# Two attention layers on one core: three edits to the planner of the instruction order

## The chip, the core and the metric

The kernel runs on one core of a Trainium2 chip. The core has a matrix engine (TensorE, PE in the profile; its weight loads are PEld), a vector engine (VectorE, DVE), a scalar engine (ScalarE, ACT), a general engine (GpSimd, POOL) and a queue engine (SyncE, SP). Each takes its own instructions strictly in the order in which the program holds them, and waits where an operand or a buffer is not ready. DMA transfers are issued by SP, ACT and POOL and run beside the engines. The metric is the device time of one execution, in microseconds (us), the median of the runs shown.

## The reference

Two attention layers of their own inputs and weights, whose outputs are joined along the last axis. Both have 2048 rows, 1024 columns and 32 heads of 32.

```python
def _A_ref(x, wqkv, wo):          # layer A
    W, dil = 8, 2
    q, k, v = ...                 # x @ wqkv, by head
    idx = pos[:, None] - (jnp.arange(W) * dil)[None, :]
    logits = einsum(q, k[idx]) * Dh ** -0.5      # 8 keys, every second one back
    logits = where(idx >= 0, logits, -1e9)
    return (softmax(logits) @ v[idx]) @ wo

def _B_ref(x, wqkv, wo):          # layer B
    W = 256
    scores = einsum(q, k) * (Dh ** -0.5)
    mask = (i - j >= 0) & (i - j < W)            # the last 256 keys
    scores = where(mask, scores, -1e9)
    return (softmax(scores) @ v) @ wo

return concatenate([A, B], axis=-1)
```

## The kernel before

**Units.** Each layer is cut into four units of 512 rows. Units 0 to 3 are layer B (dense, `DU` = 4 of them), units 4 to 7 layer A, whose even and odd rows were parted on the host so that its window is eight neighbouring keys. Every unit has eight head groups of four heads. A number (u, s) is unit and head group; `hg` = 8u + s.

**Precision.** A factor of a projection is split into a rounded part and a remainder (`Stream.parts`, L276 on ScalarE or L279 on VectorE for the rounding, L282 on VectorE for the remainder), and three products of 512 columns are summed in a PSUM bank (`TERMS`). Tiles so made are called w (weights), x (inputs) and r (sums and outputs of heads). Their raw data come through three buffers `raw`, loaded by POOL (L221); a load waits until the split of the tile three places earlier has freed its buffer. `split_to(n)` issues the splits up to item n of one long list of items, and with them the next loads.

**Layer B, attention.** A first pass (`first`) makes scores of 128 rows by 384 keys in one of four rotating PSUM banks `s`; VectorE masks them and takes the largest (L1388), ScalarE sums the exponentials (`total`, L1393), and then the bank is free. After 16 such sums their logarithm (L1406), its split (L1411 to L1414) and a small transposing matmul of `hl` with `ident` (`rows`) give 32 extra rows that are written under the queries (L1428). The second pass (`second`) computes the scores again, transposed and already normed, in the same four banks; ScalarE takes the exponentials into `pbuf` (L1473), POOL or VectorE masks them (L1452, L1455), and matmuls with V (`o<-pbuf,vbuf`) follow. The Q and K blocks are evacuated into `nat` (L625 on ScalarE, L629 on VectorE) and copied by SP into two alternating stacks `qst` and `kst` (L649), as soon as the second pass of the head group before the last has left them.

**Layer A, attention.** Scores of 32 by 40 (`s<-pbuf`), a chain on VectorE (L1214 mask, L1224 largest, L1226 subtraction, L1238 to L1242 norm, L1244 transpose) with one exponential on ScalarE between (L1230), copies into `wide` (L1253, L1256), and matmuls with V.

**Layer A, values.** Units 6 and 7 take V by seven products of half matrices (`value_product`, in the plan as "vp"), which need sums of halves of x (`sx`, items of kind "xw") and of the weights (`tv`, kind "w"). Their parts are added in VectorE out of the PSUM banks `g` (L1007); three such banks rotate. Background work (`half_sums`, L1096 to L1106) prepares these sums with DMA and VectorE while earlier units run; it begins when the last dense head group is done.

**The order.** Nothing reorders instructions later: the program's order on every engine is what a planner issues. `Clock` keeps an estimated time for each engine. A loop takes the item that can start first from four lists (sums, second pass, first pass, and `gemm`, the projections in the order of `plan`), issues its matmuls and defers what follows to an estimated moment (`ck.defer(t, f)`): work deferred to an earlier moment is issued earlier, and so stands further ahead on its engine. `e` in `first` is the estimated end of L1388 as ScalarE sees it. While `ck.traced` is set, the clock estimates loads and POOL's starts by a second model; it is set between two places in `gemm`, `marks`. In a Q/K block `run(k)` is called for k = 0 to 7, each three matmuls, and decides at which k the next items are split.

Of the kernel before, what the change touches and what calls it, by code (L numbers as in the profile page):

```python
# [55 lines left out]
BANK_LATE = 0.0  # L56
# [235 lines left out]
def kernel(ctx, tc, xs, wqk, wv, wo, outs, units):  # L292
# [4 lines left out]
    DU = sum(u[2] for u in units)  # L297
# [18 lines left out]
    ck = Clock()  # L316
# [98 lines left out]
    for p in plan:  # L415
# [21 lines left out]
        else:  # L437
# [8 lines left out]
            else:  # L446
# [6 lines left out]
    st = Stream(nc, ck, raws, wpool, xpool, items, [more[:, 1024 * i:1024 * i + 1024] for i in range(3)],  # L453
                where[("qk",) + LIGHT_FROM + (0,)] if LIGHT_FROM[0] < U else len(items))
# [76 lines left out]
    xt, xready, ot, rows, waiting = {}, {}, {}, {}, {}  # L531
# [24 lines left out]
    rg, rs, ro = Ring(psg, 7 - NS, "g"), Ring(pss, NS, "s"), Ring(pso, 1, "o")  # L556
# [7 lines left out]
    def latest(*ts):  # L564
        return None if any(t is None for t in ts) else max(ts)


    def qk_items(u, s):
# [98 lines left out]
        for t in range(2):  # L667
            h = {}

            def ready(k, t=t, h=h):  # L670
                if k == 0:
                    st.split_to(where["qk", u, s, t] + 1)
                    w = st.ready[where["qk", u, s, t]]
                    h["r"] = w if isinstance(w, list) else [w, w]
                    return latest(rg.when(), h["r"][0], xready[u][0])
                if k >= len(xready[u]):
                    return None
                if k == NK - 1 and nat + t >= NN and (dense or t == 0):
                    n = done["nat"].get(nat + t - NN)
                    return n and max(xready[u][k], n - 0.6)  # L680
                return max(xready[u][k], h["r"][k // 4])

            def run(k, t=t, h=h):
                if k == 0:
                    h["ps"], h["b"] = rg.take()
                    h["w"], _ = st.get(where["qk", u, s, t])
                for i, (a, b) in enumerate(TERMS):
                    mm(h["ps"], h["w"][:, a, k * P:(k + 1) * P], xt[u][k][:, b, :],
                                     start=(k == 0 and i == 0), stop=(k == NK - 1 and i == 2))
                then = where["qk", u, s, t] + 1  # L690
                if t == 1 and s == 0 and u:
                    then = max(then, st.split)
                kinds = [kind for kind, _ in st.items[then:then + 2]]
                if k == ASK and kinds and kinds[0] not in ("x", "xw"):
                    st.split_to(then + 1)
                if k == ASK and t == 0 and u > DU and kinds[:1] == ["x"] and st.split >= where["qk", u, s, 1]:
                    st.split_to(where["qk", u, s, 1] + 1)
                if kinds[:1] == ["xw"] and k in (0, 2, 4, 6):
                    st.split_to(then + 1 + k // 2)
                if kinds == ["w", "w"] and k == 5 and (then in firsts or then + 1 in firsts):  # L700
                    st.split_to(then + 2)
                if kinds == ["w", "xw"] and k == 6:
                    st.split_to(then + 2)
                if k in (4, 6) and kinds[:1] == ["xt"]:
                    st.split_to(then + k // 2)
                if k == 6 and t == 1 and not hg:
                    st.split_to(7)

            def after(k, t=t, h=h):
                if k == NK - 1:  # L710
                    evac(t, h["ps"], h["b"])

            for k in range(NK):
                out.append((lambda k=k, ready=ready: ready(k), lambda k=k, run=run: run(k), 3 * CG,
                            lambda k=k, after=after: after(k)))
# [644 lines left out]
    def attention(u, s):  # L1360
# [11 lines left out]
        def first(b, j):  # L1372
            if "nm" not in h:
                h["nm"] = small.tile([P, 16], F32, tag="nm", name="nm")
                h["sm"] = small.tile([P, 16], F32, tag="sm", name="sm")
            full, mask = 384, cst["mask_d"]
            cut = 0 if has_halo else max(0, 256 - P * b)
            n = full - cut
            c1 = 256 + P * b + P
            c0 = c1 - n  # L1380
            i = j * 4 + b
            ps, bank = rs.take()
            mm(ps[:, :n], q[0:96, j, b * P:(b + 1) * P], kk[0:96, j, c0:c1],
                             start=True, stop=True)
            nm, sm = h["nm"][:, i:i + 1], h["sm"][:, i:i + 1]

            def top():
                nc.vector.tensor_tensor_reduce(ps[:, :n], ps[:, :n], mask[:, cut:full], scale=-1.0, scalar=BIG,  # L1388
                                               op0=ALU.add, op1=ALU.min, accum_out=nm)
                e = ck.use("dve", n / 960 + 0.114, ck.now) + 0.06  # L1390

                def total():
                    nc.scalar.activation(ps[:, :n], ps[:, :n], AF.Exp, bias=nm, scale=-1.0, accum_out=sm)  # L1393
                    e2 = ck.use("act", n / 1200 + 0.236, e)
                    rs.give(bank, e2)
                    h["left"] -= 1
                    if h["left"] == 0:
                        ck.defer(e2, log_sum)

                ck.defer(e - 0.1, total)  # L1400

            return top

        def log_sum():
            ln = small.tile([P, 16], F32, tag="ln", name="ln")
            nc.scalar.activation(ln, h["sm"], AF.Ln)  # L1406
            e = ck.use("act", 0.13, ck.now) - 0.03

            def parts():
                nl = small.tile([P, 16], F32, tag="nl", name="nl")  # L1410
                nc.vector.tensor_tensor(nl, h["nm"], ln, op=ALU.subtract)  # L1411
                hl = small.tile([P, 2, 16], F32R, tag="hl", name="hl")
                nc.vector.tensor_copy(hl[:, 0, :], nl)
                nc.vector.tensor_tensor(hl[:, 1, :], nl, hl[:, 0, :].bitcast(F32), op=ALU.subtract)  # L1414
                e2 = ck.use("dve", 0.52, e, port=True)
                aux.append(Item(lambda: latest(rs.when(BANK_LATE), e2), lambda: rows(hl), 0.08))

            ck.defer(e, parts)

# [131 lines left out]
    aux, ones, twos, gemm = [], [], [], []  # L1551
# [6 lines left out]
    x1 = None  # L1558
    marks = []
    for p in plan:  # L1560
        if not marks and p[1] >= DU:
            marks.append(len(gemm))
        if len(marks) == 1 and p[0] == "p":
            marks.append(len(gemm))
        if p[0] == "qk":
            new = qk_items(p[1], p[2])
            if p == ("qk", 0, 0):
                q, k, x = new[:NK], new[NK:], x_items(0)
                f = dict(FILL)
                new = x[0] + sum([q[i:i + 1] + fill(i + 1, f.get(i + 1, 0)) for i in range(4)], [])  # L1570
                for i in (1, 2, 3):
                    new[new.index(q[2 * i]) if i < 2 else len(new):0] = x[i]
                    if i == 1:
                        new += k[:4]
                    else:
                        new += q[2 * i:2 * i + 2] + k[2 * i:2 * i + 2]
            if p[1:] == (0, NG - 1):
                x1 = x1 or x_items(1)
                for g in range(3, FIRST_X - 1, -1):
                    new[NK + 2 * g - 2:NK + 2 * g - 2] = x1[g]  # L1580
            gemm += new
        elif p[0] == "v":
            new = v_items(p[1], p[2])
            if p[1:] == (0, 2) and FIRST_X:
                x1 = x_items(1)
                for g in range(FIRST_X - 1, -1, -1):
                    new[X1_AT[g]:X1_AT[g]] = x1[g]
            elif V_SLOTS.get(NG - 1) == p[2] and 0 < p[1] < U - 1:
                m = 2 * VPARTS[p[2]][1]
                for g, x in reversed(list(enumerate(x_items(p[1] + 1)))):  # L1590
                    new[m * g + XAT:m * g + XAT] = x
            gemm += new
        elif p[0] == "o":
            gemm += o_items(p[1], p[2])
        elif p[0] == "p":
            gemm += product(p[1], p[2])
        elif p[0] == "vp":
            new = value_product(p[2])
            if VP_AT.get((p[1], NG - 1)) == p[2:] and p[1] + 1 < U:
                for g, x in reversed(list(enumerate(x_items(p[1] + 1)))):  # L1600
                    new[4 * g + XAT:4 * g + XAT] = x
            gemm += new
# [87 lines left out]
```

## Time and profile before

| | |
|---|---|
| median of 3 runs | 1803.5 us |
| lowest and highest | 1801.02 and 1804.85 us |
| the profiled execution's own time | 1798.77 us |
| its span | 1796.8 us |
| layer B | about 0 to 1030 us of the span |
| layer A | Q/K of its first unit from about 970 us, products of values between 1330 and 1530 us, outputs to the end |

The profile is one execution. Views read in it: the page, the waits (which engine sat idle before an instruction, and whose end released it), the time line (start, duration, engine, line, tiles, and in brackets the idle time ahead), and stretches of time with each engine's busy time. An instruction of the new order has no time there; where it would fall is read from its neighbours on the matrix engine.

### The profile page before, as it was taken

Reading aid. Unit: us, or ns where it says so; the run is one execution under the profiler, and the core shown is the slowest. Engines: PE = TensorE matmul, PEld = TensorE weight load, DVE = VectorE, ACT = ScalarE, POOL = GpSimd, SP = SyncE. Lnnn points to the kernel's source line nnn. Section 1 sums busy time; section 2 is a strip of 40 time slices with the busy share of each in tenths; the row PEclk is TensorE's granted clock in tenths of the full one; section 3 lists DMA queues with packets and bytes.
Section 4 is the critical chain, followed back from the end, with each engine's and each line's share of the span. In section 5 each row is a group of like instructions: output and inputs, shape, how many; then the busy total and the mean of one; then the engine's idle time right before and its main releaser. Section 6 shows DMA issues by size and latency. Waiting matters only on the chain.

```text
span 1796.8 us, 38440 instructions
## 1 busy us (share of the span) xinstructions
PE 1774.0 (99%) x14496; PEld 1442.6 (80%) x14496; DVE 1297.5 (72%) x2877; ACT 943.7 (53%) x2337; POOL 411.8 (23%) x961
## 2 busy tenths in 40 slices
PE   9999999999999999999999999999999999999999
PEld 7787778888778888878787788888888787887887
DVE  6777876768867769867678556766666768868866
ACT  5565566555656555656554524543464435355442
POOL 3322323222332222332223400101010101001120
PEclk9999999999999999999999999999999999999999
DMA  8354664645645556555556166766576667848984
GB/s 257 106 147 136 185 167 136 166 136 145 185 141 161 152 134 169 152 146 149 145 134 185 48 202 197 226 204 186 183 226 192 198 196 254 291 139 280 346 280 144
DMA packets 154793, 324.57 MB, mean 181 GB/s; under 512 B 18032, under 2 KB 58992, under 8 KB 154608
## 3 DMA queue, kind: packets, MB, share of 16 engines
q0 software_dynamic: 45792, 166.74, 30.5%
q1 hardware_dynamic: 98736, 137.02, 26.8%
q10 hardware_dynamic: 10080, 18.35, 2.8%
q8 instruction: 115, 1.88, 0.4%
q14 instruction: 70, 0.57, 0.1%
HBM read 201.33 MB, written 53.48 MB: 142 GB/s over the span
## 4 chain that ended last, share of the span: by engine, by line
PE 88%; DVE 4%; DMA 3%; issue 3%; ACT 1%; SPq 0%; POOL 0%; DVEq 0%; ACTq 0%; POOLq 0%
PE g L324 69%; PE s L324 13%; PE o L324 6%; DVE w L282 1%; DMA raw<-xs 1%; DMA raw<-tv 1%; DMA kst<-nat 1%; ACT s L1393 0%; DMA pbuf<-nat 0%; DVE x L282 0%; ACT w L276 0%; DVE r L1101 0%; DVE band L1242 0%; DMA qst<-nat 0%; DVE w L279 0%
## 5 line engine op out<-in xcount | busy, mean ns | idle before, releaser
L324 PE MATMUL g<-x,w 128*128 128x512 f32 x3552 | 876.2, 393 | 2.2 <-DVE w L282 0.7
L324 PEld LDWEIGHTS g<-x,w 128*128 128x128 f32 x3552 | 656.5, 188 | 131.6 <-issue 5.8
L282 DVE TENSOR_TENSOR w<-raw,w 128x512 fp32r<-128x512 f32 x510 | 334.1, 697 | 53.8 <-ACT w L276 47.3
L1393 ACT ACTIVATE s<-s,nm 128x384 f32<-128x384 f32 (+2 forms) x512 | 274.3, 537 | 118.4 <-DVE nm L1388 112.0
L1388 DVE CUSTOM_DVE_ANT_0 s<-s,mask_d 128x384 f32<-128x384 f32 (+2 forms) x512 | 261.9, 554 | 90.5 <-PE s L324 90.2
L324 PE MATMUL g<-w,x 128*128 128x256 f32 (+1 forms) x1728 | 308.9, 327 | 3.3 <-DVE w L279 1.8
L1452 POOL TENSOR_SCALAR_AFFINE_SELECT pbuf<-pbuf 128x128 f32<-128x128 f32 (+1 forms) x604 | 218.8, 390 | 315.1 <-ACT pbuf L1473 313.5
L324 PEld LDWEIGHTS g<-w,x 128*128 128x128 f32 x1728 | 256.3, 191 | 29.2 <-DVE w L282 2.7
L324 PE MATMUL g<-r,w 128*128 128x512 f32 x960 | 238.2, 393 | 0.5 <-DVE r L1352 0.5
L1473 ACT ACTIVATE pbuf<-s 128x384 f32<-128x384 f32 (+2 forms) x480 | 203.7, 504 | 62.6 <-PE s L324 60.3
L324 PEld LDWEIGHTS g<-r,w 128*128 128x128 f32 x960 | 177.3, 188 | 35.9 <-DVE r L1352 1.1
L221 POOL DMA_DIRECT2D raw<-wqk x126 | 68.1, 540 | 359.4 <-DVE w L282 241.9
L324 PEld LDWEIGHTS s<-qst,kst 128*128 128x128 f32 x704 | 113.9, 189 | 42.5 <-ACT s L1393 17.4
L324 PE MATMUL s<-kst,qst 96*128 96x384 f32 (+2 forms) x512 | 143.0, 343 | 3.5 <-DMA kst<-nat 2.6
L324 PE MATMUL s<-qst,kst 128*128 128x256 f32 (+2 forms) x704 | 137.2, 302 | 4.0 <-ACT s L1393 3.2
L276 ACT CAST w<-raw 128x1024 fp32r<-128x1024 f32 (+1 forms) x89 | 92.0, 1038 | 67.0 <-PE g L324 29.9
L279 DVE CAST w<-raw 128x1024 fp32r<-128x1024 f32 x167 | 115.7, 693 | 15.7 <-PE g L324 10.5
L324 PEld LDWEIGHTS s<-kst,qst 96*128 96x128 f32 x512 | 93.9, 189 | 29.1 <-issue 7.6
L1393 ACT ACTIVATION_READ_ACCUMULATOR s<-s,nm 128x1 f32 x512 | 105.3, 206 | 0.0
L1253 ACT COPY wide<-band 32x512 f32<-32x512 f32 x128 | 79.0, 617 | 25.0 <-DVE band L1244 23.6
L324 PE MATMUL o<-pbuf,vbuf 128*32 128x384 f32 (+2 forms) x1408 | 91.1, 388 | 0.0
L282 DVE TENSOR_TENSOR x<-raw,x 128x512 fp32r<-128x512 f32 x116 | 75.6, 689 | 21.2 <-ACT x L276 19.9
(91 smaller groups left out, 1394.1 us busy)
## 6 DMA issues: line engine op xcount, KB each, us to landing
raw<-wqk POOLq DMA_DIRECT2D x126, 512.0 KB, 4.8
raw<-wv POOLq DMA_DIRECT2D x60, 512.0 KB, 5.1
qst<-nat SPq DMA_DIRECT2D x96, 256.0 KB, 3.1
kst<-nat SPq DMA_DIRECT2D x96, 256.0 KB, 4.8
raw<-wo POOLq DMA_DIRECT2D x44, 512.0 KB, 4.5
raw<-xs POOLq DMA_DIRECT2D x28, 512.0 KB, 4.6
outs<-ost ACTq DMA_DIRECT2D x38, 256.0 KB, 2.5
kst<-halo SPq DMA_DIRECT2D x72, 128.0 KB, 4.7
```

The source lines that it names most:

```text
L221: (self.nc.scalar if early else self.nc.gpsimd).dma_start(raw if len(ap.shape) == 2 else raw.rearrange("p (a b) -> p a b", a=2), ap)
L276: nc.scalar.copy(t[:, 0, :], raw)
L279: nc.vector.tensor_copy(t[:, 0, :], raw)
L282: nc.vector.tensor_tensor(t[:, 1, c:c + 512], raw[:, c:c + 512], t[:, 0, c:c + 512].bitcast(F32), op=ALU.subtract)
L324: nc.tensor.matmul(out, left, right, **k)
L1253: nc.scalar.copy(diag[r:r + 32, :, :, c:c + 32], turned[r:r + 32, :, :, 1, :])
L1388: nc.vector.tensor_tensor_reduce(ps[:, :n], ps[:, :n], mask[:, cut:full], scale=-1.0, scalar=BIG, op0=ALU.add, op1=ALU.min, accum_out=nm)
L1393: nc.scalar.activation(ps[:, :n], ps[:, :n], AF.Exp, bias=nm, scale=-1.0, accum_out=sm)
L1452: nc.gpsimd.affine_select(w, w, pattern=[[0, m], [step, n]], compare_op=ALU.is_ge, fill=0.0, base=base, channel_multiplier=chan)
L1473: nc.scalar.activation(w, ps[:, :pack * n].rearrange("p (j n) -> p j n", j=pack), AF.Exp)
```

## The change

```diff
@@ in qk_items, run(k) @@
-                if kinds[:1] == ["xw"] and k in (0, 2, 4, 6):
-                    st.split_to(then + 1 + k // 2)
+                if kinds[:1] == ["xw"] and k in (0, 2, 4):
+                    st.split_to(then + 2 + k // 2)
...
-                if kinds == ["w", "xw"] and k == 6:
+                if kinds == ["w", "xw"] and k == 3:
                     st.split_to(then + 2)
@@ in attention, first @@
-                ck.defer(e - 0.1, total)
+                ck.defer(e - 0.7, total)
@@ in attention, log_sum @@
-                aux.append(Item(lambda: latest(rs.when(BANK_LATE), e2), lambda: rows(hl), 0.08))
+                aux.append(Item(lambda: latest(rs.when(BANK_LATE), e2 + 0.4), lambda: rows(hl), 0.08))
@@ in the main part @@
-        if not marks and p[1] >= DU:
+        if not marks and p[1:] == (DU, 2) and p[0] == "qk":
             marks.append(len(gemm))
```

1. Ahead of a value product, the last Q/K block splits the product's items at k = 0, 2 and 4, two at the first of these, instead of one each at 0, 2, 4 and 6; where the next items are one weight and then such a sum, they are split at k = 3 instead of 6.
2. The summing exponential is deferred to 0.7 us ahead of the estimated end of L1388, instead of 0.1.
3. The transposing matmul of the sums may be issued 0.4 us later by the planner's clock.
4. The second model of the clock begins with the third Q/K block of unit 4, not with the first entry of the plan that belongs to that unit.

The matmuls are the same and as many. On ScalarE stand 14 instructions fewer than before, on VectorE 13 fewer, on POOL 27 more: casts and masks that the planner gave to another engine. SP's order is the same. The matrix engine's order is the same up to about 43 us, from about 1030 to 1405 us and from about 1550 us on; between these it differs in many places. Three follow, as the built programs hold them. Names are output<-inputs, with the numbers of the buffers.

**First place: a second pass of the dense layer beside the first pass of the next head group, at 448 to 455 us before (it comes again 256 us later in each dense unit).** The matrix engine, before:

```order
L324 MATMUL g_4881<-x_4855,w_4700 128x512 x3
L324 MATMUL g_4881<-x_4858,w_4700 128x512 x3
L324 MATMUL s_4955<-qst1_124,kst1_126 128x384
L324 MATMUL s_4957<-qst1_124,kst1_126 128x256 x2
L324 MATMUL s_4961<-qst1_124,kst1_126 128x256 x2
L324 MATMUL s_4965<-qst1_124,kst1_126 128x128 x2
L324 MATMUL s_4971<-qst1_124,kst1_126 128x128 x2
L324 MATMUL g_4985<-x_4704,w_4950 128x512 x3
L324 MATMUL s_4994<-kst0_125,qst0_123 128x384
```

and with the change:

```order
L324 MATMUL s_4932<-qst1_124,kst1_126 128x256 x2
L324 MATMUL g_4898<-x_4868,w_4712 128x512 x3
L324 MATMUL s_4946<-qst1_124,kst1_126 128x128 x2
L324 MATMUL s_4950<-qst1_124,kst1_126 128x128 x2
L324 MATMUL s_4954<-kst0_125,qst0_123 128x384
L324 MATMUL g_4898<-x_4871,w_4712 128x512 x3
L324 MATMUL s_4979<-kst0_125,qst0_123 128x384
L324 MATMUL s_4981<-kst0_125,qst0_123 128x384
L324 MATMUL s_4987<-kst0_125,qst0_123 128x384
L324 MATMUL s_4991<-kst0_125,qst0_123 128x384
```

The Q block's last product (g_4881, now g_4898) moved behind the second pass, and four first-pass matmuls follow it at once; s_4987 takes the bank of s_4950, and s_4991 that of s_4954. ScalarE there, before:

```order
L1473 ACTIVATE pbuf_110<-s_4929 128x384
L1473 ACTIVATE pbuf_110<-s_4932 128x384
L625 ACTIVATE nat_4943<-g_4881 128x512
L1393 ACTIVATE s_4897,sm_4643<-s_4897,nm_4642 128x384
L1473 ACTIVATE pbuf_110<-s_4955 128x384
```

and with the change:

```order
L1473 ACTIVATE pbuf_110<-s_4946 128x2x128
L625 ACTIVATE nat_4970<-g_4898 128x512
L1473 ACTIVATE pbuf_110<-s_4950 128x2x128
L1393 ACTIVATE s_4954,sm_4650<-s_4954,nm_4649 128x384
L1393 ACTIVATE s_4979,sm_4650<-s_4979,nm_4649 128x384
```

The evacuation L625 stands ahead of the summing exponential in both.

**Second place: VectorE ahead of the fifth value product, at 1422 to 1434 us before.** r_15951 and r_15954 (now r_15933 and r_15936) are the first sums of x, w_16012 (now w_15996) is the product's second weight. Before:

```order
L1224 TENSOR_REDUCE nm_15924<-band_10854 128x16
L1226 TENSOR_TENSOR band_10854<-band_10854,nm_15924 128x16x40
L1238 TENSOR_REDUCE sm_15940<-band_10854 128x16
L1240 RECIPROCAL sm_15940<-sm_15940 128x16
L1242 TENSOR_TENSOR band_10854<-band_10854,sm_15940 128x16x40
L1244 STREAM_TRANSPOSE band_10854<-band_10854 128x1024
L282 TENSOR_TENSOR r_15951<-raw_15759,r_15951 128x512
L282 TENSOR_TENSOR r_15954<-raw_15759,r_15954 128x512
L279 CAST w_15984<-raw_15821 128x1024
```

and with the change, from the second half of the first sums on:

```order
L282 TENSOR_TENSOR r_15936<-raw_15756,r_15936 128x512
L1224 TENSOR_REDUCE nm_15942<-band_10883 128x16
L1226 TENSOR_TENSOR band_10883<-band_10883,nm_15942 128x16x40
L279 CAST w_15966<-raw_15832 128x1024
L282 TENSOR_TENSOR w_15966<-raw_15832,w_15966 128x512 x2
L1238 TENSOR_REDUCE sm_15974<-band_10883 128x16
L1240 RECIPROCAL sm_15974<-sm_15974 128x16
L1242 TENSOR_TENSOR band_10883<-band_10883,sm_15974 128x16x40
L1244 STREAM_TRANSPOSE band_10883<-band_10883 128x1024
L282 TENSOR_TENSOR r_15982<-raw_15841,r_15982 128x512
L282 TENSOR_TENSOR r_15985<-raw_15841,r_15985 128x512
L282 TENSOR_TENSOR w_15996<-raw_15951,w_15996 128x512 x2
```

The split of the first sums moved from behind the window's softmax to ahead of it, and the first weight into its middle.

**Third place: ScalarE ahead of the last value product, at 1517 to 1525 us before.** w_17124 is that product's first weight. Before:

```order
L1326 COPY r_11650<-o_17077 128x512
L1037 DMA vd_108<-r_15148 128x512
L586 ACTIVATE nat_17105<-g_17041 128x512
L276 CAST w_17124<-raw_17048 128x1024
L1230 ACTIVATE band_11127<-band_11127 128x16x40
L591 COPY nat_17105<-g_17112 128x512
```

and with the change:

```order
L586 ACTIVATE nat_17083<-g_17035 128x512
L1037 DMA vd_108<-r_15148 128x512
L1326 COPY r_11650<-o_17093 128x512
L1230 ACTIVATE band_11132<-band_11132 128x16x40
L591 COPY nat_17083<-g_17113 128x512
```

The cast of w_17124 left ScalarE; it stands on VectorE now (L279), between L1226 and L1238 of the same window.

## The prediction

> **What bounds the kernel now.** I read the page's head first, then the waits of the matrix engine (PE), then the stretches of 100 us, then the time line at each wait.
>
> ```profile
> span 1796.8 us, 38440 instructions
> PE 1774.0 (99%) x14496; PEld 1442.6 (80%) x14496; DVE 1297.5 (72%) x2877; ACT 943.7 (53%) x2337; POOL 411.8 (23%) x961
> ```
>
> PE is busy for all but 22.8 us. The number of its instructions does not change, so a new order can win or lose only what PE waits, and the slow clock that follows some waits. The waits by releaser (total, times, longest):
>
> ```profile
> PE s L324 <- ACT s L1393: 4.5, 7, 1.0
> PE g L324 <- DVE w L282: 3.5, 7, 1.3
> PE s L324 <- DMA kst<-nat: 2.6, 1, 2.6
> PE g L324 <- DVE w L279: 1.8, 1, 1.8
> ```
>
> So four kinds carry it: score banks that ScalarE's summing exponential (L1393) holds, weight splits of VectorE in layer A, one key copy by DMA, one late cast. By stretch (PE, PEld, DVE, ACT, POOL, clock, DMA share, GB/s):
>
> ```profile
> 100.00:200.00 100.00, 98.17 (x584) 79.52 (x583) 78.96 (x218) 54.65 (x170) 30.06 (x72) 0.98 0.50 140
> 900.00:1000.00 100.00, 96.79 (x621) 81.41 (x621) 74.50 (x181) 51.97 (x151) 30.11 (x72) 0.98 0.52 140
> 1500.00:1600.00 100.00, 97.34 (x1189) 78.01 (x1188) 75.49 (x124) 47.47 (x89) 9.52 (x18) 1.00 0.75 251
> ```
>
> The worst stretches are the dense layer's first unit, the passage to layer A, and layer A's products of values: the three that the edits reorder.
>
> **A. The split of sums earlier (L698 to L703).** It adds no work; it issues the same splits of layer A's value products two to three steps of a Q/K block earlier, thus also the loads behind them. A 128x512 matmul takes 0.23 us from start to start (30 in 7.09 us in the first row). The products' waits:
>
> ```profile
> 1515.60 7.09 PE L324 MATMUL g<-x,w 128*128 128x512 f32 x30
> 1427.90 0.72 POOL L221 DMA_DIRECT2D raw<-wv  x1 [7.55 <-DVE r L282]
> 1431.93 1.05 ACT L276 CAST w<-raw 128x1024 fp32r<-128x1024 f32 x1 [0.56 <-DMA raw<-wv]
> 1433.03 0.50 PE L324 MATMUL g<-w,r 128*128 128x512 f32 x1
> 1434.36 1.88 PE L324 MATMUL g<-w,r 128*128 128x512 f32 x7 [0.83 <-DVE w L282]
> 1380.44 1.05 ACT L276 CAST w<-raw 128x1024 fp32r<-128x1024 f32 x1 [0.52 <-DMA raw<-tv]
> ```
>
> At 1433 us PE loses 1434.36 - 1433.03 - 0.23 = 1.1 us. The chain runs back to POOL: its load of the last weight waited 7.55 us for a buffer which the split of r (L282) frees, and VectorE had that split behind a whole softmax (reduce to transpose). In the new order it stands ahead of the first reduce, four softmax rows earlier, so the load leaves some 4 us sooner and the weight is no longer what is late; VectorE's last subtraction is, by about 0.3 us (it now stands behind the transpose). Saved: 0.8. At 1380 us the late thing is the landing of raw<-tv; its request keeps its place on POOL, so that wait stays.
>
> ```profile
> 1510.29 4.33 PE L324 MATMUL g<-x,w 128*128 128x512 f32 x18 [0.65 <-DVE r L1007]
> 1519.67 1.05 ACT L276 CAST w<-raw 128x1024 fp32r<-128x1024 f32 x1 [1.78 <-DMA raw<-tv]
> 1520.62 0.73 ACT L1230 ACTIVATE band<-band 128x640 f32<-128x640 f32 x1
> 1525.12 0.65 DVE L279 CAST w<-raw 128x1024 fp32r<-128x1024 f32 x1
> 1522.53 1.52 PE L324 MATMUL g<-w,x 128*128 128x512 f32 x6
> 1525.83 0.49 PE L324 MATMUL g<-w,x 128*128 128x512 f32 x1 [1.78 <-DVE w L279]
> 1526.55 1.67 PE L324 MATMUL g<-w,x 128*128 128x512 f32 x6 [0.23 <-DVE w L282]
> ```
>
> At 1510 PE waited 0.65 us for a bank that VectorE empties (L1007); that row moves ahead of the softmax: saved 0.7. At 1525 the loss is 1525.83 - 1522.53 - 6 x 0.23 = 1.9, then 1526.55 - 1525.83 - 0.23 = 0.5, so 2.4. Here ScalarE held the window's exponential (L1230) behind a cast that waited 1.78 us for DMA; in the new order the cast goes to VectorE and the exponential is free. VectorE's cast at 1525.12 then comes about 1.9 us sooner, but PE arrives 0.8 sooner too: 1.1 saved. What is late next is the same cast. A: -0.8 - 0.7 - 1.1 = -2.6; between 0 (the splits wait for landings all the same) and -4.2 (all three gone).
>
> **B. The passage to layer A.** The exponentials' move and the later switch of the planner's clock re-plan 930 to 1030 us; from there to 1370 us every engine's order is the old one, so the switch costs nothing in layer A itself.
>
> ```profile
> 966.60 0.72 POOL L221 DMA_DIRECT2D raw<-wv  x1 [2.12 <-DVE pbuf L1455]
> 968.81 2.61 SPq L649 DMA_DIRECT2D kst<-nat  x3
> 971.47 4.39 SPq L1096 DMA_DIRECT2D r<-wv  x4
> 974.00:976.00 2.00, 2.00 (x11) 1.65 (x10) 1.70 (x4) 0.97 (x4) 0.80 (x1) 1.00 1.10 225
> 982.45 1.22 PE L324 MATMUL s<-kst,qst 96*128 96x384 f32 x3 [2.60 <-DMA kst<-nat]
> 982.00:984.00 2.00, 1.55 (x5) 1.49 (x6) 1.94 (x4) 0.00 (x0) 0.30 (x1) 0.63 1.02 382
> 983.47 2.92 PE L324 MATMUL g<-w,x 128*128 128x512 f32 x7
> ```
>
> The last head's key copies are issued at 968.8 and land only at 982.4, because the DMA engines are full (share 1.10). PE waits 2.60 us; then the granted clock is 0.63 and seven matmuls take 2.92 instead of 1.6, 1.3 more: 3.9 in all. In the new order PE's work between the last use of the old keys and the first use of the new ones, counted in matmuls of the times above, is 13.8 us instead of 12.6, and two of the weight loads that share the engines are asked for some 4 us of PE work earlier. If the copies land as late as now relative to their issue, 1.2 of the wait goes and 1.4 and part of the slow clock stay; if the loads are out of the way, all goes. I take -2.4, between -3.9 and +0.7 (PE comes 0.7 us of work earlier, and nothing else moves).
> The Trainium skill (TensorE: Matmul & The Clock Gate, Why this matters for your kernels) says that throughput drops after PE gaps above about 3 us. By that rule the slow clock would not follow a wait of 2.60; this trace shows it, and after one of 0.97 below, so the measurement decides. By the rule B would be worth at most 2.6.
>
> **C. The dense layer's first unit.** The exponential (L1393) is queued 0.6 us of planner time sooner, and the transposing matmul of the sums (L1416) is asked for 0.4 later.
>
> ```profile
> 166.20 1.30 ACT L720 COPY vbuf<-g 128x512 f32<-128x512 f32 x2 [4.03 <-PE g L324]
> 167.40 0.46 ACT L1393 ACTIVATE s<-s,nm 128x256 f32<-128x256 f32 x1
> 168.02 1.84 PE L324 MATMUL s<-qst,kst 128*128 128x384 f32 x4 [0.97 <-ACT s L1393]
> 171.23 1.48 PE L324 MATMUL g<-x,w 128*128 128x512 f32 x3
> 194.74 1.90 PE L324 MATMUL s<-qst,kst 128*128 128x384 f32 x5 [0.42 <-ACT s L1393]
> ```
>
> At 167 us two copies (1.30) stand ahead of the exponential whose bank PE needs: 0.97 lost, and three matmuls in 1.48 instead of 0.7 show the slow clock, about 2.5 in all. The new order has one copy ahead, but again two exponentials late one after the other; I get waits of some 0.9 and 1.0, so -0.5. At 194.7 five score matmuls of 0.18 take 1.90 after a wait of 0.42: 1.4 lost; in the new order no score bank is taken again that soon there. C: -1.9, between -3.9 and +2 (both losses again, elsewhere).
>
> **D. The other dense units** repeat each other.
>
> ```profile
> 451.78 0.60 ACT L625 ACTIVATE nat<-g 128x512 fp32r<-128x512 f32 x1 [0.66 <-PE g L324]
> 452.28 0.55 ACT L1393 ACTIVATE s<-s,nm 128x384 f32<-128x384 f32 x1
> 452.99 0.82 PE L324 MATMUL s<-qst,kst 128*128 128x128 f32 x4 [0.61 <-ACT s L1393]
> 461.57 0.22 PE L324 MATMUL s<-ident,hl 128*32 128x128 f32 x1 [0.31 <-DVE hl L1414]
> ```
>
> Here the edit does not do what it says: the evacuation L625, which waits for PE, still stands ahead of the exponential, now with a small one between. The third of four score matmuls then waits for L625 (0.60) and 0.3 of that one, some 0.8; the fourth 0.55 more for the exponential: 1.35 instead of 0.75, in three units: +1.8. The wait of 0.31 at 461.57 (twice) goes with the later request: -0.6. D: +1.2, between -2.9 (all gone) and +3.
>
> Sum: -2.6 - 2.4 - 1.9 + 1.2 = -5.7 us. The profiled execution took 1798.77 (span 1796.8 and 2.0 around it) and would come to 1793.1; it lay 4.7 under the median of the runs shown, 1803.5, so I set the sum against that median: **1797.8**.
>
> **Rivals.**
> 1. The waits only move. For it: D, the wait at 1380, and that banks taken again within 2.0 us of PE work number 19 in the new order, 20 in the old. Against it: the order of A is better at three named waits. With A at half (-1.3), B and C at nothing, D +1.2: 1803.4.
> The Trainium skill (DMA: Bandwidth & Descriptors, Issuing engines are not separate DMA queues) says that requests of all engines run on the same 16 DMA engines and interleave. The row at 974 (share 1.10) agrees: asking sooner adds no bandwidth.
> 2. ScalarE blocks, and it is slower. Exponentials queued 0.6 us sooner wait for VectorE at the head of ScalarE's queue, and the second pass's exponentials, evacuations and casts wait behind them; PE then misses score banks.
>
> ```profile
> L1393 ACT ACTIVATE s<-s,nm 128x384 f32<-128x384 f32 (+2 forms) x512 | 274.3, 537 | 118.4 <-DVE nm L1388 112.0
> ```
>
> For it: ScalarE already sits idle 118.4 us ahead of these 512. Against: it is only 55% busy at 100 to 200 us. If one wait more of 0.6, as in D, falls in each of 16 of the 32 heads, that is +9.6; with the sum it gives 1807.4. It decides the sign from 10 heads on.
>
> **How the numbers follow.** Forecast 0.62, rival 1 0.20, rival 2 0.18. A change under 0.2% (3.6 us) cannot be told from none. The forecast's own range is 1794.7 (A and B at their best) to 1800.2 (B at nothing). The range of all, 1790 to 1808, reaches up to rival 2's price and leaves out what lies beyond, and below it all four parts at their best (1788.6). Faster 0.61 (of the forecast's 0.62 a little lies within 0.2%), same 0.21 (rival 1 and that rest), slower 0.18 (rival 2).
>
> **What would show it.** Right: no wait on kst<-nat above 1 us and a clock of 1.00 at 980 to 990; no wait at 1510, and under 1.5 us lost at 1525; waits on L1393 of more than 1 us at some 450, 700 and 960 us. Wrong: PE's idle time at 900 to 1000 as now, or ScalarE's idle ahead of L1393 far above 118 with new PE waits on L1473.

## The result and the profile after

Over twelve runs the changed kernel takes 1798.89 us (1795.8 to 1801.52), the kernel before beside it 1803.68: a ratio of 0.9972 with a 95% interval of 0.9963 to 0.998, so 0.28% or some 5 us faster. The forecast was 1797.8. The two executions that were profiled differ by nothing (1798.99 against 1798.77), because that of the kernel before lay 5 us below its median; so where the time came from has to be read from several profiles, and the experiments gave twelve more.

The head of the page after the change:

```profile
span 1797.3 us, 38398 instructions
PE 1774.6 (99%) x14496; PEld 1443.4 (80%) x14496; DVE 1297.6 (72%) x2864; ACT 939.1 (52%) x2323; POOL 446.0 (25%) x988
```

The waits of the matrix engine after the change (us in total, times, longest):

```profile
PE g L324 <- DVE w L282: 3.1, 4, 2.2
PE g L324 <- DVE r L1352: 2.7, 2, 1.4
PE s L324 <- DMA kst<-halo: 2.4, 1, 2.4
PE o L324 <- issue: 2.0, 2, 1.0
PE s L324 <- ACT pbuf L1473: 1.8, 3, 0.6
PE s L324 <- ACT s L1393: 1.7, 5, 0.4
```

The wait on kst<-nat (2.6) is gone, that on the late cast L279 fell from 1.8 to 0.2, those on L1393 from 4.5 to 1.7. Three kinds are new: kst<-halo, L1473, and waits of matmuls into `o` for which the profile shows no releaser ("issue"); those on L1352 grew from 0.5 to 2.7. By stretch after the change (PE, PEld, DVE, ACT, POOL, clock, DMA share, GB/s):

```profile
100.00:200.00 100.00, 99.48 (x624) 80.51 (x623) 83.44 (x228) 57.43 (x179) 38.42 (x81) 1.00 0.51 145
200.00:300.00 100.00, 97.38 (x533) 76.27 (x526) 74.27 (x200) 58.45 (x174) 25.89 (x63) 0.98 0.60 162
500.00:550.00 50.00, 48.63 (x301) 37.92 (x300) 34.68 (x92) 33.20 (x95) 18.32 (x50) 1.00 0.49 143
900.00:1000.00 100.00, 98.88 (x623) 83.75 (x622) 78.92 (x195) 51.21 (x148) 30.03 (x65) 1.00 0.52 148
1300.00:1400.00 100.00, 96.86 (x1236) 80.03 (x1236) 67.25 (x121) 52.18 (x94) 12.71 (x24) 0.98 0.64 199
1400.00:1500.00 100.00, 100.00 (x1155) 80.63 (x1154) 72.87 (x132) 47.30 (x93) 12.04 (x22) 1.00 0.65 203
1500.00:1600.00 100.00, 99.54 (x1225) 79.71 (x1224) 78.36 (x128) 47.32 (x89) 9.53 (x18) 1.00 0.75 253
```

Four stretches of the kernel before that the prediction did not show:

```profile
200.00:300.00 100.00, 98.87 (x564) 76.65 (x564) 75.20 (x206) 61.78 (x183) 28.27 (x73) 1.00 0.60 166
500.00:550.00 50.00, 49.77 (x306) 38.39 (x306) 33.03 (x79) 29.76 (x84) 20.72 (x48) 1.00 0.50 144
1300.00:1400.00 100.00, 98.21 (x1250) 81.61 (x1249) 69.86 (x125) 52.47 (x96) 12.71 (x24) 1.00 0.66 207
1400.00:1500.00 100.00, 98.89 (x1173) 79.11 (x1172) 71.77 (x130) 48.19 (x93) 12.04 (x22) 1.00 0.64 195
```

PE's busy time rose at 100 to 200, 900 to 1000 and 1400 to 1600 us, the places the prediction named. It fell at 200 to 300, 500 to 550 and 1300 to 1400, which it did not.

### The profile page after: what moved, and what is told of

Read it like the earlier page. It is cut to its first block, busy times and chain, and to the rows that moved or that the text cites. A ratio compares the mean times of both kernels' runs of the same rounds, so it can differ in the third digit from the quotient of the medians.

```text
span 1797.3 us, 38398 instructions
## 1 busy us (share of the span) xinstructions
PE 1774.6 (99%) x14496; PEld 1443.4 (80%) x14496; DVE 1297.6 (72%) x2864; ACT 939.1 (52%) x2323; POOL 446.0 (25%) x988
## 4 chain that ended last, share of the span: by engine, by line
PE 89%; DVE 5%; DMA 3%; ACT 1%; issue 1%; POOL 0%; SPq 0%; DVEq 0%; ACTq 0%
PE g L324 70%; PE s L324 12%; PE o L324 7%; DVE w L282 1%; DMA raw<-xs 1%; DMA raw<-tv 1%; DMA od<-r 1%; DVE x L282 1%; ACT pbuf L1473 0%; DMA pbuf<-nat 0%; DMA kst<-halo 0%; DVE s L1388 0%; DVE w L279 0%; ACT s L1393 0%; POOL pbuf L1452 0%
## 5 line engine op out<-in xcount | busy, mean ns | idle before, releaser
L282 DVE TENSOR_TENSOR w<-raw,w 128x512 fp32r<-128x512 f32 x510 | 338.2, 705 | 48.1 <-ACT w L276 42.1
L1393 ACT ACTIVATE s<-s,nm 128x384 f32<-128x384 f32 (+2 forms) x512 | 273.6, 535 | 163.4 <-DVE nm L1388 162.5
L1452 POOL TENSOR_SCALAR_AFFINE_SELECT pbuf<-pbuf 128x128 f32<-128x128 f32 (+1 forms) x631 | 253.1, 429 | 336.2 <-ACT pbuf L1473 331.4
L1388 DVE CUSTOM_DVE_ANT_0 s<-s,mask_d 128x384 f32<-128x384 f32 (+2 forms) x512 | 262.1, 552 | 96.5 <-PE s L324 95.3
L1473 ACT ACTIVATE pbuf<-s 128x384 f32<-128x384 f32 (+2 forms) x480 | 202.4, 502 | 100.9 <-PE s L324 99.2
L279 DVE CAST w<-raw 128x1024 fp32r<-128x1024 f32 x169 | 117.2, 693 | 17.2 <-PE g L324 16.0
L1393 ACT ACTIVATION_READ_ACCUMULATOR s<-s,nm 128x1 f32 x512 | 104.0, 203 | 0.0
L1428 DVE TENSOR_TENSOR qst<-s,pick 32x512 fp32r<-32x512 f32 x128 | 79.3, 676 | 24.9 <-PE s L324 24.5
L221 POOL DMA_DIRECT2D raw<-wv x60 | 39.5, 658 | 219.8 <-DVE w L282 153.0
```

Of the source, the lines that this page charges most:

```text
L221: (self.nc.scalar if early else self.nc.gpsimd).dma_start(raw if len(ap.shape) == 2 else raw.rearrange("p (a b) -> p a b", a=2), ap)
L279: nc.vector.tensor_copy(t[:, 0, :], raw)
L282: nc.vector.tensor_tensor(t[:, 1, c:c + 512], raw[:, c:c + 512], t[:, 0, c:c + 512].bitcast(F32), op=ALU.subtract)
L1428: nc.vector.tensor_tensor(q[96:P, j, :].rearrange("p (b s) -> p b s", s=P), ps[0:32, None, 0:P].to_broadcast([32, 4, P]), cst["pick"][0:32 ...
L1452: nc.gpsimd.affine_select(w, w, pattern=[[0, m], [step, n]], compare_op=ALU.is_ge, fill=0.0, base=base, channel_multiplier=chan)
L1473: nc.scalar.activation(w, ps[:, :pack * n].rearrange("p (j n) -> p j n", j=pack), AF.Exp)
```

## The experiments

Each was run beside the kernel before on one chip. **Theory:** edit 1 pays in the value products, edits 2 to 4 by planning layer B anew. **Rivals:** the waits only move; ScalarE blocks; the difference is that of one execution from the next.

**One edit at a time**, on the kernel before:

```diff
e1_splits:  kinds[:1] == ["xw"] and k in (0, 2, 4): st.split_to(then + 2 + k // 2)
            kinds == ["w", "xw"] and k == 3:        st.split_to(then + 2)
e2_expo:    ck.defer(e - 0.7, total)
e3_rows:    aux.append(Item(lambda: latest(rs.when(BANK_LATE), e2 + 0.4), ...
e4_mark:    if not marks and p[1:] == (DU, 2) and p[0] == "qk":
```

> The kernel before with edit 1 alone (the splits ahead of the value products two to three steps earlier). Theory (the terms add, each edit pays at its own places): PE's losses in the value products go as between the two traces, 1.1 us at 1433, 0.7 at 1510 and some 1.6 at 1525, so -2.6 to -3.4 us, a ratio of 0.9981 to 0.9986, and layer B as before (the wait on kst<-nat at 982 stays). Rival 1 (waits only move): the loads land no sooner, one of the three waits comes back at the next cast, -1.3 us or less, ratio 0.9993 or more. Rival 3 (the gain is not of the edits' places but of the runs' variation at DMA waits): no change.

Measured: 1797.01 us, ratio 0.996 (0.9945 to 0.9975). Edit 1 alone gains as much as the whole change or more, and more than the theory gave it (0.9981 to 0.9986 lies outside the interval).

> The kernel before with edit 2 alone (the summing exponential deferred to 0.7 us ahead of the estimated end of its VectorE pass). Theory: it carries the cost in the dense units 1 to 3 (waits on L1393 and L1473 of 1.1 us together near 450, 709 and 968, and the waits of 1.65 on VectorE's L1352 near 519 and 777 if they are of its order), and the gain in the first unit; the passage to layer A changes only in part without edit 4. I expect -1 to +2 us, ratio 0.9995 to 1.001, with ScalarE's idle ahead of L1393 near 163 us instead of 118. Rival 2 (ScalarE blocks): +5 us or more, ratio above 1.0027, hidden in the full change by the other three edits. Rival (the exponentials' move is itself the gain): -3 us or less.

Measured: 1805.24, ratio 1.001 (0.9995 to 1.0025), ScalarE's idle time ahead of L1393 161.7 us. As the theory had it in size; but the waits on L1352 near 519 and 777 are not in its profile, so they belong to the edits together.

> The kernel before with edit 3 alone (the transposing matmul of the sums asked for 0.4 us later). Theory: only the waits on hl by that matmul go, 0.3 to 0.5 us each, two or three of them, and the first unit is re-ordered: -0.6 us, between -1.5 and +1, ratio 0.999 to 1.0005. Rival (the first unit's re-ordering is the whole gain of the dense layer): -2 us or less.

Measured: 1814.99, ratio 1.0063 (1.0039 to 1.0088). Both theories missed: four tenths of a microsecond of planner's time, alone, cost 11 us. Its profile has a wait of 3.3 us near 208, of 2.2 near 725 and of 4.2 near 991 that the kernel before has not or has smaller.

> The kernel before with edit 4 alone (the planner's second model begins with unit 4's third Q/K block). Theory: the passage is planned anew, the key copies get more PE work between old and new keys, the wait of 2.6 us on kst<-nat and the slow clock behind it go wholly or for the most part: -2.4 to -3.9 us, ratio 0.9978 to 0.9987; the layer A Q/K blocks up to 1330 us, which this edit alone orders anew, cost nothing. Rival 1: the copies land as late and the wait stays above 1 us, -1 us or less. Rival 4 (layer A needs the second model from its first entry on): new waits between 1010 and 1330 us, above 0.

Measured: 1803.36, ratio 0.9993 (0.998 to 1.0006). The wait on kst<-nat is gone from the profile as the theory said, but a wait of 3.1 us on a weight near 1161 came in the re-ordered Q/K blocks of layer A: rival 4.

By their ratios the four edits would add up to 0.9960 + 1.0010 + 1.0063 + 0.9993 - 3 = 1.0026, slower; together they give 0.9972. Edits 2 and 3 change the same planned order, and they do not act alike: on top of edits 1, 2 and 4, edit 3 does no harm at all (1798.89 with it, 1800.2 without, by the runs below), while edit 2 costs some 6 us on top of edits 1 and 4, of which edit 3 takes back about one.

**Some edits together:**

```diff
e5_no_splits:   the changed kernel, edit 1 undone    (edits 2, 3, 4)
e6_splits_mark: the changed kernel, 2 and 3 undone   (edits 1, 4)
e7_no_rows:     the changed kernel, edit 3 undone    (edits 1, 2, 4)
e8_no_mark:     the changed kernel, edit 4 undone    (edits 1, 2, 3)
```

> The changed kernel without edit 1 (edits 2, 3 and 4 together; the value products in the old order). Theory now (edit 1, which alone measured 0.996, is the whole gain, and B, C and D of the prediction sum to about nothing or a loss): 0 to +2 us against before, ratio 1.000 to 1.0015. The prediction's own sum (B -2.4, C -1.9, D +1.2): -3.1 us, ratio 0.9983. If the single edits added up (+2.0 of edit 2, +11.8 of edit 3, -1.3 of edit 4): +12 us, ratio 1.007.

Measured: 1803.18, ratio 0.9998 (0.9989 to 1.0007). Edits 2 to 4 together are worth nothing; the prediction's -3.1 for them (0.9983) lies outside the interval.

> The kernel before with edits 1 and 4 alone. Theory (both pay at their own places, edit 1 -6.2, edit 4 -1.3 by the ratios measured alone): -7 to -8 us, ratio 0.9955 to 0.9962, and better than the change as it is. Rival (edit 4's passage gains 4 us and gives 3 back in a wait on a weight near 1161 us, which the profile with edit 4 alone shows as 3.13 us): as edit 1 alone, 0.996 to 0.9968.

Measured: 1793.82, ratio 0.9946 (0.9932 to 0.9959): better than the change by some 5 us.

> The changed kernel without edit 3 (edits 1, 2 and 4). Theory (edit 3 only counters what edit 2 does to the order: alone each costs, together they are about even): slower than the change by 1 to 4 us, ratio to before 0.9975 to 0.9995, with the waits on L1393 of edit 2 alone at 453, 470, 714 and 730 us in its profile. Rival (edits add; edit 3 costs 11.8 alone): faster than the change by several us, ratio 0.993 or less.

Measured: 1800.2, ratio 0.998 (0.9967 to 0.9994), with the waits on L1393 at 451, 466, 712 and 729 us. As the theory had it, though only 1.3 us above the change, and the two intervals overlap.

> The changed kernel without edit 4 (edits 1, 2 and 3). Layer B's order is that of the change up to about 930 us, so this prices the passage alone. Prediction's term B, as far as it hangs on the switch of the clock: the wait on kst<-nat near 980 comes back, 2 to 4 us slower than the change, ratio to before 0.9983 to 0.9995. Rival (the passage is worth nothing; in other draws of the old order the same copies land sooner): within 1 us of the change, ratio 0.9968 to 0.9978.

Measured: 1798.4, ratio 0.9964 (0.9951 to 0.9978), and no wait on kst<-nat near 980. The rival holds: in the change the switch of the clock brings nothing to the whole. Edits 2 and 3 re-plan the passage by themselves: in this profile it takes only 0.4 us more than in the change's. The run prices more than the passage, though, since without edit 4 the order between 1050 and 1200 us differs as well; a wait of 1 us that the change has at 1077 is not there.

**Where in edit 1, where in edit 4, and the dose of edit 2:**

```diff
e9_half_sums:    kinds[:1] == ["xw"] and k in (0, 2, 4): st.split_to(then + 2 + k // 2)
e10_half_weight: kinds == ["w", "xw"] and k == 3:        st.split_to(then + 2)
e11_mark_qk1:    edit 1, and  if not marks and p[1:] == (DU, 1) and p[0] == "qk":
e12_expo_13:     edits 1 and 4, and  ck.defer(e - 1.3, total)
```

> The kernel before with the first half of edit 1 alone (the product's items split at k = 0, 2, 4, two at the first; the rule for a weight and then a sum stays at k = 6). Theory: this half holds the wait at 1433 us (its chain began with the split of the first sum, behind a softmax) and the cast that is late near 1525; with the window rule read from the nine profiles so far (a 3.41-us window in which PE idles 2.1 us or more is followed by one at half clock, below 1.75 never) it also saves part of the slow clock. -3 to -5 us, ratio 0.9972 to 0.9984. Rival (the halves need each other): within 1 us of before. The window rule's own test in this profile: no half clock without a window of 1.75 us idle ahead of it, and none missing behind 2.1.

Measured: 1798.6, ratio 0.9969 (0.9958 to 0.9981), a little beyond the theory. The waits at 1433 and near 1525 are gone from its profile.

> The kernel before with the second half of edit 1 alone (a weight and then a sum: split at k = 3 instead of 6). Theory: it holds the wait of 0.7 us near 1510 and little else: -0.5 to -1.5 us, ratio 0.9992 to 0.9997. Rival: it carries half of the gain or more, -3 us, 0.9983. The window rule as above.

Measured: 1798.28, ratio 0.9966 (0.9952 to 0.9979). The rival holds: the second half alone gains as much as the first, and the halves do not add, since both together gave 0.996. Its profile has no wait at 1433 any more either, but still a late cast near 1523; the first half's has two new waits of 1.0 and 1.6 near 1405 and 1514. How the gain divides stays open: by the value products' time in one profile each (161.6 and 163.3 us, table below) the halves are worth 2.1 and 0.4, by the runs 5 each.

> Edits 1 and 4, with the second model beginning one Q/K block sooner (unit 4's second). The order then differs from that of edit 1 alone only in the passage, about 930 to 985 us; layer A's Q/K blocks stand as before the change. Theory (edit 4 pays in the passage): the wait on kst<-nat near 979 is gone, the 2.70 us near 1159 that edits 1 and 4 show is gone too, and the wait near 1340 (1.5 to 2.35 in all profiles of the old order, nothing with edits 1 and 4) is back: within 1.5 us of edits 1 and 4, ratio 0.994 to 0.9957. Rival (edit 4's gain lies in layer A's new order): as edit 1 alone, 0.996 to 0.997.

Measured: 1791.94, ratio 0.9937 (0.9924 to 0.995), the fastest of all. The head of this kernel's page:

```profile
span 1788.3 us, 38453 instructions
```

The top of its waits:

```profile
PE s L324 <- ACT s L1393: 4.6, 7, 1.0
PE g L324 <- DVE w L282: 2.4, 4, 1.5
PE s L324 <- DVE qst L1606: 1.5, 1, 1.5
```

Neither kst<-nat nor L279 is in the list, and the longest wait is 1.5 us. Only the passage is planned otherwise than with edit 1 alone, and the gain against edit 1 alone is 4 to 5 us (0.9937 against 0.996; 1791.94 against 1797.01): it lies in the passage, as the theory had it. In the profiles the stretch from 932 to 1044 us is 3.2 us shorter than with edit 1 alone.

> Edits 1 and 4, with the summing exponential deferred to 1.3 us ahead of the estimated end of VectorE's pass (edit 2 has 0.7, the kernel before 0.1). On this base 0.1 gave 1793.8 us and 0.7 gave 1800.2. Rival 2 of the prediction (ScalarE blocks at the head of its queue, each exponential queued too early holds it): the cost grows with the dose, to 1806 us or more (ratio 1.0015 and above), and ScalarE's idle ahead of L1393 goes beyond 220 us. Theory (the edit only deals the order of the dense layer anew, a few places of 0.5 to 1.7 us in each unit): no order in the dose, 1796 to 1803 us, ratio 0.996 to 0.9998. The window rule as above.

Measured: 1804.81, ratio 1.0011 (1.0001 to 1.0021). The top of its waits:

```profile
PE g L324 <- DVE w L282: 6.9, 10, 2.2
PE s L324 <- ACT s L1393: 6.2, 12, 1.0
PE s L324 <- DVE hl L1414: 1.8, 2, 1.4
```

Its page's row of the summing exponential:

```profile
L1393 ACT ACTIVATE s<-s,nm 128x384 f32<-128x384 f32 (+2 forms) x512 | 272.8, 533 | 187.6 <-DVE nm L1388 183.1
```

The time lies between what the two theories expected, and it does rise with the dose: 1793.8 at 0.1, 1800.2 at 0.7, 1804.8 at 1.3. The theory's "no order in the dose" is wrong. ScalarE's idle time ahead of L1393 rises with the dose too, 109.1, 163.3 and 187.6 us in the three profiles, but stays below the 220 that blocking was to bring, and the waits are spread: ten on weights, twelve on banks. So the earlier exponentials cost, some 6 and 11 us on the base of edits 1 and 4, in a few places of each unit; that ScalarE's blocked queue is the cause of all of them is not shown.

## Why the prediction was right, and where it was not

Its time and its sign came true. Its terms did not: one was too small, one had far too little loss in it, and these errors cancelled. That the sum came within 1.1 us of the result is luck: by the runs, edits 2 to 4 were worth about nothing where -3.1 was forecast, and edit 1 some -4 to -6 where -2.6 was. Two stages can be compared in all profiles, since the same matmul begins and ends them (in the kernel before at 43.2, 1392.8 and 1555.5 us):

| profiles | 43 to 1393 us | 1393 to 1556 us (value products) |
|---|---|---|
| before | 1349.6 | 162.8 |
| edit 1; its halves | 1349.9; 1348.4, 1349.3 | 159.0; 161.6, 163.3 |
| change | 1353.9 | 158.7 |
| change without edit 1; without edit 4 | 1353.1; 1353.3 | 162.6; 159.0 |
| edit 2; edit 3; edit 4 | 1358.7; 1364.3; 1353.3 | 162.8; 164.4; 165.7 |
| edits 1 and 4; with the earlier mark | 1348.5; 1345.1 | 159.3; 158.8 |
| edits 1, 2, 4; with the dose 1.3 | 1355.8; 1361.8 | 158.5; 158.7 |

**A was mis-sized: -2.6 forecast, -4.8 measured.** Without edit 1 the value products take 162.6 to 165.7 us (five profiles, mean 163.7), with it 158.5 to 159.3 (seven, mean 158.9). All three places went as described, and each by more than its term: 1.1 at 1433, 0.8 at 1510, and at 1525, after the change:

```profile
1524.32 1.52 PE L324 MATMUL g<-w,x 128*128 128x512 f32 x6
1526.02 0.50 PE L324 MATMUL g<-w,x 128*128 128x512 f32 x1 [0.18 <-DVE w L279]
1526.75 3.49 PE L324 MATMUL g<-w,x 128*128 128x512 f32 x14 [0.23 <-DVE w L282]
```

1526.02 - 1524.32 - 6 x 0.227 = 0.3 and then 0.5 are lost there instead of 1.9 and 0.5. That makes -3.5; the two profiles differ by -4.1 in all. The rest is that the forecast sized these waits by the one execution at hand, and in others the old order pays more. With edit 4 alone, whose value products stand in the old order, PE lost 3.0 us at the cast near 1530, and the clock halved behind it (stretches, columns as above):

```profile
1526.00:1532.00 6.00, 2.90 (x12) 1.84 (x11) 5.86 (x9) 2.77 (x7) 0.53 (x1) 1.00 0.88 317
1532.20:1535.60 3.40, 3.40 (x9) 2.66 (x9) 2.09 (x4) 1.63 (x4) 0.53 (x1) 0.50 0.91 298
```

**B was right in mechanism, and in size with some luck.** From here on I compare the starts of matmuls at which both orders have issued the same work, as means over the profiles with the new layer B (the change, and it without edit 1 or 4) against those with the old (before, edit 1, its halves). From 932 to 1044 us the new order is 2.4 us shorter, as forecast. Of the two ways given, the second came: the loads are out of the way. The prediction gave that way the full 3.9, and -2.4 was its compromise between the two, so the match in size is partly luck: the wait and the slow clock went, and against the profile before that is -2.9, since D's new loss of 0.55 us at 954 and some 0.5 more at 969 stand in the same stretch. After the change the key copies' issue, POOL's next load and the first use stand so in the time line:

```profile
969.45 1.87 SPq L649 DMA_DIRECT2D kst<-nat  x3
971.19 0.72 POOL L221 DMA_DIRECT2D raw<-wv  x1 [1.44 <-DVE w L282]
...
982.81 0.86 PE L324 MATMUL s<-kst,qst 96*128 96x384 f32 x4
```

The copies' time from issue to landing, by the view of the DMA:

```profile
DMA to landing us min/median/max: 4.6/4.9/5.3
```

The load of wv that was asked for 2.2 us ahead of the copies (966.60) is now asked for 1.7 behind them, and the copies land 5 us after issue; in the kernel before PE got them 13.6 us after the first issue (968.81 to 982.45). The clock at 900 to 1000 is 1.00. What failed is the cause: the switch of the clock (edit 4) is not needed for it in the change, as the run without it showed.

**C: -1.9 forecast, -1.3 measured** from 151 to 264 us, and that is mostly the slow clock: the old order itself had it at 170 us in two of its four profiles, and the other two (edit 1, its first half) take 1.5 us less there than the kernel before, as the change does (1.3). The waits at 167 and 194.7 shrank or went; what came instead was no bank of scores but a key copy at 208 us, with the rows of PE there:

```profile
201.61 3.65 SPq L580 DMA_DIRECT2D kst<-halo  x3
...
210.55 0.30 PE L324 MATMUL s<-kst,qst 96*128 96x128 f32 x1 [2.44 <-DMA kst<-halo]
210.97 3.29 PE L324 MATMUL g<-w,x 128*128 128x512 f32 x9
```

PE now comes to the keys of the halo before their copy, issued from 201.6 us on, has landed, and waits 2.4; behind it nine matmuls take 3.29 instead of 9 x 0.227 = 2.0.

**D is the step that failed: +1.2 forecast for three units, +5.5 measured in the first two of them alone, outside its own bound of +3.** That is the difference from 420 to 853 us. The place that the prediction priced behaved as it said: the evacuation still stands ahead, and PE loses 0.8 to a small exponential and 0.4 to the large one behind it (1.35 forecast), and the waits on hl are gone. The sign named for it, waits on L1393 of more than 1 us, did not come, since PE waits for L1473 there and on L1393 never longer than 0.4:

```profile
452.40 1.00 PE L324 MATMUL s<-kst,qst 96*128 96x384 f32 x2 [0.61 <-ACT pbuf L1473]
```

But it took these two places for the whole unit. The time line after the change at 519 us, and again 258 us later:

```profile
519.81 0.60 DVE L1388 CUSTOM_DVE_ANT_0 s<-s,mask_d 128x384 f32<-128x384 f32 x1
520.33 0.68 DVE L1352 TENSOR_TENSOR r<-o,r 128x512 fp32r<-128x512 f32 x1
521.07 1.19 PE L324 MATMUL g<-r,w 128*128 128x512 f32 x4 [1.37 <-DVE r L1352]
```

Three passes of L1388 for four score blocks, which PE now issues at once behind the products with V, stand ahead of the sum's remainder L1352; in the old order it came first there. The output product then loses 1.65 us instead of 0.5. In the runs without edit 1 and without edit 4 the clock also halved behind the place at 519, 1.6 us more. A loss of 0.55 at 437, 695 and 954 us (0.39 of it idle, behind L1393) is new too.

**Outside the terms** there is +2.8 from 1044 to 1393 us, where the change keeps the old order. About 1.1 of it is the wait without a releaser at 1077 (0.98 us of idle time in the change, 1.37 without edit 1, none without edit 4). Most of the rest is the weight near 1341:

```profile
1344.19 5.09 PE L324 MATMUL g<-w,x 128*128 128x512 f32 x14 [2.19 <-DVE w L282]
```

The idle time there is 2.16 to 2.19 us in the three new profiles against 1.17 to 2.17 in the four with the old layer B, so not clearly longer; but in two of the three new ones the clock halved behind it, and in none of the old. Neither cause was tried.

Together: by profiles layer B and the passage lose 4.1 us (1353.4 against 1349.3, means of three and four) where -3.1 was forecast, and the value products win 4.8. By the runs, edits 2 to 4 are worth -0.1 (without edit 1) and +1.9 (1798.89 against 1797.01 with it). The two measures differ by 2 to 4 us, and at least half of that has a place. One stretch of slow clock lowers the mean granted clock by 0.00095. The profiles show half a stretch to one too few with the old layer B (before: 0.9976 against 0.9971 in 29 runs; edit 1: 0.9990 against 0.9980) and about half a stretch too many with the new one (the change: 0.9977 against 0.9983), some 2 to 3 us together.

**Rivals.** "The waits only move" describes edits 2 to 4 well (0.9998), and not edit 1. "ScalarE blocks": ScalarE's idle time went from 118 to 163 us and new waits on L1473 came, the signs it named; the price of edits 2 and 3 on top of edits 1 and 4 is 1798.89 - 1793.82 = 5.1 us, half of the 9.6 that the rival had priced.

```profile
L1393 ACT ACTIVATE s<-s,nm 128x384 f32<-128x384 f32 (+2 forms) x512 | 273.6, 535 | 163.4 <-DVE nm L1388 162.5
```

A cost of that sign was there, and edit 1 outweighed it; that ScalarE's queue made all of it is not shown, as the wait on VectorE's L1352 is another.

## What to carry to other kernels

Constants of a planner do not add: each deals the whole order anew, so run them apart and together before keeping any; here two of four edits were better left out, and edits 1 and 4 with the mark one Q/K block sooner run 12 us below the kernel before instead of 5. Price a wait from several executions, since one execution can lie 5 us off its median, as that of the kernel before did. When a place in a repeating unit is priced, read the rest of the unit's order too, above all the queue of the engine that comes next (VectorE's here).

## What was not expected of the hardware

The slow clock follows a rule that the prediction did not have. In the profiles, but for the stretch that runs past the end, it comes in stretches of 3.413 us (twice two in a row) at a clock of 0.50, and within a profile they lie on one grid of that length to 0.01 us. I cut all fourteen profiles by their grid and took PE's idle time in each piece from the starts of its matmuls and their usual durations (leaving out the first 12 us, the end, and pieces that are slow themselves):

| idle in a piece of 3.41 us | pieces | followed by a piece at half clock |
|---|---|---|
| 2.07 us and more | 19 | 19 |
| 1.80 to 2.07 | 20 | 11 |
| 0.80 to 1.80 | 192 | 0 |

The bound near 2 us hangs on the durations taken for layer A's smallest matmuls: counted by intervals between starts alone, five pieces of 2.07 to 2.43 us in layer A had no slow piece behind them. Below 1.8 us no piece had one either way.

Half clock takes 1.7 of the 3.41 us. So a wait of 2.3 us costs 2.3 where the grid cuts it in two, and 4.0 where it lies in one piece: the key copy near 980 us cost PE 2.23 us of idle time with edit 1 alone, with no slow stretch behind it, and 2.29 with its first half alone, with one; at 167 us the wait of 0.97 and small losses around it made 2.1 in one piece. The expectations of three of the last four runs held this rule, and their profiles kept to it; the bounds of the table were drawn afterwards, from all of them. Its grid does not begin with the kernel (the first edges differ from profile to profile), which is probably a good part of why runs of one program differ: the kernel before took, in the median by its clock over 72 runs, 1797.5 us at 1.000 (1 run), 1798.9 at 0.999 (5), 1801.0 at 0.998 (17), 1803.6 at 0.997 (28), 1805.2 at 0.996 (17) and 1808.1 at 0.995 (4). Of the 9.2 us between 0.999 and 0.995, the clock itself makes 0.004 x 1800 = 7.2; that the place of the grid sets it in each run is argued, not shown. The fastest kernel's profile has no such stretch before its end. The Trainium skill (TensorE: Matmul & The Clock Gate, What's actually happening) describes a free-running window of 3413 ns and half clock after an idle window; the length and the grid agree with these rows, but here some 2 us of idle time in a window were enough.
